# Handing out a triangular substitution's operations behind other VectorE operations, in a linear-attention kernel followed by two feed-forward layers

## The chip, the cores and the metric

One core of one Trainium2 chip runs the whole program in a single launch. The metric is the device time of one execution in microseconds (us). The engines that matter here are TensorE (PE: matmuls and, as PEld, the loading of their weights), VectorE (DVE), ScalarE (ACT), GpSimd (POOL) and SyncE (SP, which issues most DMAs). Each engine runs its own list of instructions in order and waits on semaphores for the others.

## The reference

The program computes three stages on fp32 data, cut here to what is computed:

```python
# attention: batch 4 x 8 heads, 768 positions, head size 40
for t in range(S):
    y[:, :, t] = einsum('bhd,bhde->bhe', rt, state)
    Sa = einsum('bhde,bhe->bhd', state, at)
    state = state*wt[:, :, None, :] - einsum('bhd,bhe->bhde', Sa, bt)
    state = state + einsum('bhd,bhe->bhde', vt, kt)
# mixture of experts: 3072 tokens x 320, 8 experts of width 1024, the best one of each token
h = maximum(x[mask] @ w1[e], 0);  out[mask] = gate_w * sigmoid(x @ w_output_gate)[e] * (h @ w2[e])
# shared layer of width 2048
h = x @ w_in;  g = maximum(h,0) + alpha*minimum(h,0);  out = g @ w_out
```

## The kernel before, in words

**Attention in chunks.** The recurrence is done in 12 chunks of 64 positions, and each chunk in two halves of the heads: 24 steps (`NST=24`), each for 8 groups of heads on 128 partitions. `slot(s)` writes the instructions of step s, for s from 0 to 24. Within a chunk the term `Sa` depends on earlier positions of the same chunk, so each step needs the inverse of a unit lower triangular matrix. The kernel inverts its two 32x32 diagonal blocks and joins them by matmuls.

**What is prepared ahead.** `LA=8` steps before a step runs, `stepA1` and `stepA1b` prepare its operands on VectorE: two scans over 520 columns (`F`, L604, and `e`, L610), a reciprocal and a copy of 8 columns (L607, L608), and two products (`kf`, 1024 columns, L614; `g`, 512 columns, L619). TensorE then forms `L` from them (L628). ScalarE evicts the parts of `L` to be inverted into `nt` (L633, L634), and VectorE the masked rest into `ka` (L636; `kx` in some steps, which is the same thing).

**The substitution.** Every fourth step `inv_push` (L656) takes the four steps that are complete and inverts all of their blocks at once. A stream transpose (L659) puts the blocks into `S`, so that each partition holds one 32x32 matrix. Then 30 operations `op(j)`, j from 30 down to 1, eliminate one column each: a product into `tmp` (L673, `mul` below) and an addition into `S` (L674, `add` below) over j(31-j) columns, 30 to 240. The addition needs the product, and the next operation's product needs the addition. Where j(31-j) is above 70, product and addition are each cut into two halves of rows, so that a half's successor is not the instruction that needs it. A last stream transpose writes the result `tt` (L677). Six groups of four steps are inverted: group 0 before step 0, group 1 pushed in step 0, and groups 2 to 5 at the end of steps 3, 7, 11 and 15. A group's result is first used four steps later at most, by the matmuls `W` (L744).

**How its operations are dealt out before.** `inv(n)` (L649) is called at fixed places of a step with shares from `NI=[0,1,4,1,1]`; each call issues its share of the operations that are left, all of them behind each other. In a step the places are: behind the first `W` (where s is no multiple of 4), between the two parts of the recurrence's output and the second `W` (two calls), and at the step's end.

**The rest of a step on the engines' lists.** TensorE runs, in order: `R` (L733), the transposes `XT` (L762), a part of `MY` (L772), the first `W`, the first `Pp` (L776), `R` again (L796), the second `Pp`, `MTp` (L804), the second `W`, then `MY` (L816) in two parts, of which the second needs the second `x`. Behind them come, in two of four steps, the transposes `xtp` of the finished positions (L123), and then `R` (L692), `kbp` (L642) and `L` (L628) for later steps. VectorE runs: the two `x` products from the two `Pp` (L777), some substitution operations, the state update `tm` and `mc` (L719, L720), the two output products `yt` (L821), where there is an `xtp` its small sums `lg` (L124), then `stepA1`, `stepA1b`, `ka`. ScalarE evicts `xtp` into `xu` (behind `lg`), then `kbp` into `kb`, which the next step's `R` (L733) waits for. In steps 17 to 24 no operand is prepared any more.

**What follows.** The attention's output is routed to experts while the recurrence runs, and the two feed-forward layers follow on TensorE (`hp`, L390, and `yp`, L417) from about 400 us to the end.

## Time and profile before

| | |
|---|---|
| runs, us | 1007.9, 1003.08, 1009.45 (median 1007.9) |
| profiled execution, us | 1002.83 (span of its trace 1001.1) |
| mean granted TensorE clock | 0.971 of full speed |
| TensorE busy | 938.4 us (94%) |
| VectorE busy | 778.5 us (78%), 1898 instructions |
| ScalarE busy | 397.8 us (40%) |
| chain that ended last | PE 66%, DVE 22%, DMA 5%, issue 4%, ACT 2% |

The busy shares are means over stages with different limits: attention with its prelude fills about the first 400 us of the span, the two layers the rest. The chain that ended last is followed back from the last instruction; a line's share in it says how much of the span that line's work stood on the path that set the end. In timelines one row is a run of equal instructions: start, time from the first's start to the last's end, engine, line, output<-inputs, partitions x columns, count, and in brackets how long the engine was idle before and who ended it. Since instructions overlap, the difference of two rows' starts is what the first one costs its engine.

### The profile page before, as it was taken

The page shows a single profiled execution, that of the slowest core. Times are in us where ns is not written, and L with a number is a line of the kernel's source. Part 1 is how long each engine was busy: PE and PEld are TensorE (multiplying, and loading weights), DVE is VectorE, ACT ScalarE, POOL GpSimd, SP SyncE. Part 2 cuts the span into 40 slices and gives each one's busy share as a digit, 9 for nine tenths or more (in the row PEclk, how much of TensorE's full clock was granted, in tenths as well). Part 3 has the DMA queues.
Part 4 walks back from the last instruction along what each step waited for, and adds up shares of the span by engine and source line. Part 5 has one row for each costly group of instructions (what it writes and reads, how often), then busy time and mean ns, then how long its engine had stood idle before and what let it go on. Part 6 is the DMA issues. An engine that isn't in the chain of part 4 may idle for free.

```text
span 1001.1 us, 26895 instructions
## 1 busy us (share of the span) xinstructions
PE 938.4 (94%) x11172; PEld 855.0 (85%) x11172; DVE 778.5 (78%) x1898; ACT 397.8 (40%) x816; POOL 155.0 (15%) x242
## 2 busy tenths in 40 slices
PE   5368999899999999999999999899999999999998
PEld 5367888788888898999999999778999999999997
DVE  7999999999988835788888886677666666666654
ACT  3734545445453344465555655332121212212111
POOL 1000000101110113414444443301001010100000
PEclk8568999999999999999999999999999999999999
DMA  4333867444441364467777767420001000000000
GB/s 129 117 102 103 251 215 230 117 122 126 115 118 54 97 189 130 165 231 246 226 238 230 218 230 229 146 87 27 27 1 53 1 27 27 27 27 1 28 1 26
DMA packets 59391, 118.46 MB, mean 118 GB/s; under 512 B 7492, under 2 KB 34308, under 8 KB 59268
## 3 DMA queue, kind: packets, MB, share of 16 engines
q1 hardware_dynamic: 55220, 103.04, 33.6%
q0 software_dynamic: 4048, 13.69, 4.1%
q8 instruction: 88, 1.44, 0.6%
q14 instruction: 35, 0.29, 0.1%
HBM read 90.24 MB, written 26.46 MB: 117 GB/s over the span
## 4 chain that ended last, share of the span: by engine, by line
PE 66%; DVE 22%; DMA 5%; issue 4%; ACT 2%; POOL 0%; SPq 0%; DVEq 0%; ACTq 0%; POOLq 0%
PE hp L390 24%; PE yp L417 24%; DVE S L674 4%; DVE tmp L673 4%; PE MY L816 3%; PE Pp L776 3%; DVE F L604 2%; DVE kf L614 2%; PE tp L379 2%; PE W L744 2%; DVE x L777 1%; PE MY L772 1%; DVE w L306 1%; PE R L733 1%; PE xtp L123 1%
## 5 line engine op out<-in xcount | busy, mean ns | idle before, releaser
L390 PE MATMUL hp<-xh,w 128*128 128x512 f32 (+3 forms) x1008 | 298.4, 379 | 0.1
L417 PE MATMUL yp<-w,hh 128*128 128x320 f32 (+1 forms) x1280 | 284.4, 309 | 1.0 <-ACT hh L406 0.6
L417 PEld LDWEIGHTS yp<-w,hh 128*128 128x128 f32 (+1 forms) x1280 | 217.0, 186 | 12.9 <-ACT hh L406 2.3
L390 PEld LDWEIGHTS hp<-xh,w 128*128 128x128 f32 x1008 | 187.4, 188 | 25.8 <-issue 0.4
L417 PE MATMUL yp<-w,hl 128*128 128x320 f32 x584 | 181.4, 311 | 4.1 <-DVE hl L398 3.0
L406 ACT CAST hh<-g 128x512 fp32r<-128x512 f32 x96 | 59.5, 620 | 275.4 <-PE yp L417 148.3
L390 PE MATMUL hp<-xl,w 128*128 128x512 f32 (+3 forms) x336 | 126.1, 375 | 0.2 <-DVE xl L382 0.2
L407 DVE TENSOR_TENSOR hl<-g,hh 128x512 fp32r<-128x512 f32 x96 | 66.5, 692 | 72.8 <-ACT hh L406 72.8
L417 PEld LDWEIGHTS yp<-w,hl 128*128 128x128 f32 x584 | 109.7, 188 | 6.7 <-DVE hl L398 3.8
L404 DVE TENSOR_SCALAR g<-hp,al 128x512 f32<-128x512 f32 x96 | 71.9, 749 | 39.7 <-PE hp L390 39.7
L306 DVE TENSOR_TENSOR w<-raw,w 128x1024 fp32r<-128x1024 f32 (+3 forms) x65 | 88.5, 1363 | 15.8 <-ACT w L305 14.0
L674 DVE TENSOR_TENSOR S<-S,tmp 128x110 f32<-128x110 f32 (+19 forms) x336 | 69.7, 246 | 0.8
L673 DVE TENSOR_TENSOR tmp<-S 128x110 f32<-128x110 f32 (+19 forms) x336 | 69.4, 245 | 0.5
L405 DVE SCALAR_TENSOR_TENSOR g<-hp,g 128x512 f32<-128x512 f32 x96 | 66.4, 692 | 3.3
L390 PEld LDWEIGHTS hp<-xl,w 128*128 128x128 f32 x336 | 63.4, 189 | 5.4 <-DVE xl L382 0.6
L305 ACT CAST w<-raw 128x1024 fp32r<-128x1024 f32 (+1 forms) x66 | 64.2, 974 | 5.5 <-DMA raw<-W 5.5
L504 POOL DMA_INDIRECT xg<-xs,pos x24 | 25.5, 1062 | 226.8 <-PE tp L379 167.6
L776 PE MATMUL Pp<-rz,xt 128*128 128x128 f32 x384 | 55.3, 287 | 0.0
L816 PE MATMUL MY<-x,kb 128*64 128x104 f32 (+1 forms) x768 | 43.7, 255 | 10.4 <-DVE x L777 10.4
L747 ACT COPY x<-W 32x320 f32<-32x320 f32 x96 | 40.0, 416 | 29.9 <-PE W L744 27.2
L395 ACT ACTIVATE hh<-hp 128x448 fp32r<-128x448 f32 (+2 forms) x72 | 36.6, 508 | 37.2 <-issue 25.0
L816 PEld LDWEIGHTS MY<-x,kb 128*64 128x64 f32 x768 | 36.7, 140 | 14.1 <-DVE x L777 13.0
(171 smaller groups left out, 1376.9 us busy)
## 6 DMA issues: line engine op xcount, KB each, us to landing
raw<-W SPq DMA_DIRECT2D x45, 512.0 KB
x<-VX SPq DMA_DIRECT2D x48, 232.0 KB
fm<-FM SPq DMA_DIRECT2D x46, 160.0 KB
xs<-z SPq DMA_DIRECT2D x5, 1440.0 KB
raw<-WI SPq DMA_DIRECT2D x10, 512.0 KB
raw<-WO SPq DMA_DIRECT2D x10, 512.0 KB
vv<-VM SPq DMA_DIRECT2D x24, 160.0 KB
rz<-R SPq DMA_DIRECT2D x48, 80.0 KB
```

The costliest lines, as they stand in the source:

```text
L305: s.nc.scalar.copy(hi,r[0][:,0:n])
L306: (eng or s.nc.vector).tensor_tensor(lo,r[0][:,0:n],hi.bitcast(F32),SUB)
L390: for i,(l,r) in enumerate(seq): nc.tensor.matmul(hp,l,r,start=(i==0),stop=(i==len(seq)-1))
L404: nc.vector.tensor_scalar(g,hp,0.0,s.al[:,f:f+1],ALU.min,MUL)
L405: nc.vector.scalar_tensor_tensor(g,hp,0.0,g,ALU.max,ADD)
L406: nc.scalar.copy(hh,g)
L407: nc.vector.tensor_tensor(hl,g,hh.bitcast(F32),SUB)
L417: nc.tensor.matmul(yp[j][o],l,r[:,f],start=(f==0 and i==0),stop=(f==nf-1 and i==len(p)-1))
L673: V.tensor_tensor(t3[:,r],S[:,r,j:j+1].to_broadcast([P,n,w]),S[:,j:j+1,j+1:].to_broadcast([P,n,w]),MUL)
L674: for r in rows: V.tensor_tensor(S[:,r,j+1:],S[:,r,j+1:],t3[:,r],ADD)
L776: nc.tensor.matmul(Pp[:,2*qq:2*qq+2],xt[:,qq,128*sd:128*sd+128],rz1[:,:,qq,sd],start=True,stop=True)
L816: nc.tensor.matmul(MY[q//4][64*sd:64*sd+64,q//2%2,104*(q%2)+o:104*(q%2)+o+w1],kb1[:,q,64*sd:64*sd+64],x1[:,sd,q//2,128*(q%2)+o:128*(q%2)+o ...
```

## The change

- `op(j)` no longer issues its instructions. It returns two functions, `mul` and `add`, which issue the product and the addition either in halves, as before, or whole.
- A new function `tick()` takes the next of these functions and issues it whole. It is called behind VectorE operations of other kinds: four times in `stepA1` (behind `F`, behind the copy, behind `e`, behind `kf`), once in `stepA1b` (behind `g`), behind `ka`, behind the state update `mc`, behind each `yt` and behind each `x`. These are 11 calls per step; where nothing is left to hand out, a call does nothing.
- What the calls of the remaining steps can't take, `due(r)` issues in halves, at one place per step between the second `x` and the state update, where before the two calls of `inv` stood; in the fourth step of a group it issues all that is left. The first steps of the prelude call `inv(4)` in place of `inv(8)`, since the calls of `tick` take a part there as well.
- The last group (pushed at the end of step 15) keeps halves and shares: `left[0]=25` turns `tick` off, and `share` issues 5, 2 and 1 shares at three places of a step, where before the calls of `inv` had 1+4, 1+1 and 1. In three of its four steps the single share moves behind the second `R`, `x` and `rh`.

The number of `tmp` and `S` instructions per group was 112 in all six; it is now 94, 80, 78, 78, 78 and 112, which is 152 fewer of 672. The columns that they work on are the same. The lists of TensorE, ScalarE, GpSimd and SyncE hold the same rows in the same order as before.

The core of the diff:

```diff
         nc.vector.tensor_tensor_scan(F[:,519::-1],f[:,520:0:-1],ones1.rearrange("p q t -> p (q t)")[:,::-1],0.0,MUL,ADD)
         F3=F[:,0:520].rearrange("p (q t) -> p q t",q=8)
+        tick()
...
         nc.vector.tensor_copy(e64,F3[:,:,0:1])
+        tick()
         e=ring.tile([P,8,65],F32,tag="e",name="e",bufs=LA+2)
...
+        tick()
         if s in (1,3,5): kf=xt.rearrange("p a (b h t) -> p (a b) h t",b=2,h=2)
...
         KF[s]=kf;E[s]=e;E64[s]=e64
+        tick()
...
         nc.vector.tensor_tensor(g,A3,e[:,:,0:64],MUL)
+        tick()
...
-    left=[1]; WARM=12
+    invq=deque(); fine=[]; end=[]; WARM=12
+    def tick():
+        if left[0]: return
+        if not fine and invq: fine.extend(invq.popleft())
+        if fine: fine.pop(0)(False)
     def inv(n):
-
-        l=max(left[0],n,1) if n<100 else n
-        left[0]-=n
-        for _ in range(-(-len(invq)*n//l)): invq.popleft()()
+        while fine: fine.pop(0)(False)
+        for _ in range(min(n,len(invq))):
+            for f in invq.popleft(): f(True)
         if not invq and end: end.pop()()
-    end=[]
+    def due(r): inv(100 if r==3 else max(0,-(-(len(invq)-11*(3-r)//2)//(4-r))))
+    left=[0]
+    def share(n):
+        l=max(left[0],n,1); left[0]-=n
+        inv(-(-len(invq)*n//l))
...
-            w=31-j
-            t3=ep.tile([P,240],F32,tag="tmp",name="tmp",bufs=2)[:,0:j*w].rearrange("p (a b) -> p a b",a=j)
-
-            rows=[slice(j//2,j),slice(0,j//2)] if j*w>70 else [slice(0,j)]
-            for r in rows:
-                n=r.stop-r.start
-                V.tensor_tensor(t3[:,r],S[:,r,j:j+1].to_broadcast([P,n,w]),S[:,j:j+1,j+1:].to_broadcast([P,n,w]),MUL)
-            for r in rows: V.tensor_tensor(S[:,r,j+1:],S[:,r,j+1:],t3[:,r],ADD)
+            w=31-j; t3=[]
+            def parts(split): return [slice(j//2,j),slice(0,j//2)] if split and j*w>70 else [slice(0,j)]
+            def mul(split):
+                t3.append(ep.tile([P,240],F32,tag="tmp",name="tmp",bufs=2)[:,0:j*w].rearrange("p (a b) -> p a b",a=j))
+                for r in parts(split):
+                    n=r.stop-r.start
+                    V.tensor_tensor(t3[0][:,r],S[:,r,j:j+1].to_broadcast([P,n,w]),S[:,j:j+1,j+1:].to_broadcast([P,n,w]),MUL)
+            def add(split):
+                for r in parts(split): V.tensor_tensor(S[:,r,j+1:],S[:,r,j+1:],t3[0][:,r],ADD)
+            return [mul,add]
...
-        for j in range(30,0,-1): invq.append(lambda j=j: op(j))
+        for j in range(30,0,-1): invq.append(op(j))
...
-        inv(NI[0])
         if B: wmm(0)
...
-        if s%4: inv(NI[1])
...
+        if s>=LATE and s%4: share(1)
         if Y: pp(1)
...
-        inv(NI[1])
-        inv(NI[2])
+        if s<LATE: due(s%4)
+        else: share(5)
         if B: wmm(1)
...
         if n2 is not None: a2ka(n2)
-        inv(NI[3])
+        if s>=LATE: share(2)
         if n2 is not None: loadAn()
-        inv(NI[4])
-
-        if n2 is not None and n2%4==3: inv_push(n2//4)
+        if n2 is not None and n2%4==3:
+            inv_push(n2//4)
+            if s+1==LATE: left[0]=25
```

`LATE` is 16. The other calls of `tick` stand behind `ka` (`a2ka`), behind the state update (`state`), behind each `x` (`pp`) and behind each `yt` (in `slot`); in the prelude `inv(8)` becomes `inv(4)` at two places.

How the list of VectorE moves, at the end of step 8 (the first of a group's four), from the state update to `ka`. In these rows `tmp` and `S` are the substitution's, and the numbers behind names are buffers. Before:

```order
L719 TENSOR_TENSOR tm<-MY,mc_117 128x160 x2
L720 TENSOR_TENSOR mc_117<-tm,e_1160 128x8x40
L821 TENSOR_TENSOR yt<-MY,e 128x4x64 x2
L124 TENSOR_REDUCE lg<-xtp 128x16 x2
L604 SCALAR_TENSOR_TENSOR F<-fm_91,ones_92 128x520
L607 RECIPROCAL d_93<-F 128x8
L608 COPY e_3417<-F 128x8
L610 SCALAR_TENSOR_TENSOR e<-fm_91,d_93 128x520
L614 TENSOR_TENSOR kf<-fm_91,F 128x1024
```

This stretch held no substitution operation; seven of them stood ahead of `tm`, and four more follow behind `ka`.

The same stretch of VectorE's list now:

```order
L734 TENSOR_TENSOR tm<-MY,mc_117 128x160 x2
L735 TENSOR_TENSOR mc_117<-tm,e_1129 128x8x40
L686 TENSOR_TENSOR tmp<-S 128x150
L837 TENSOR_TENSOR yt<-MY,e 128x4x64
L688 TENSOR_TENSOR S<-S,tmp 128x25x6
L837 TENSOR_TENSOR yt<-MY,e 128x4x64
L686 TENSOR_TENSOR tmp<-S 128x168
L124 TENSOR_REDUCE lg<-xtp 128x16 x2
L604 SCALAR_TENSOR_TENSOR F<-fm_91,ones_92 128x520
L688 TENSOR_TENSOR S<-S,tmp 128x24x7
L608 RECIPROCAL d_93<-F 128x8
L609 COPY e_3329<-F 128x8
```

Whole products and additions stand one by one between the others: three of them are ahead of `lg` and `F`, where none was.

VectorE's list further on, in step 9, around the two `x` products (`ez` and `sc` belong to the routing). Before:

```order
L673 TENSOR_TENSOR tmp<-S 128x110 x2
L674 TENSOR_TENSOR S<-S,tmp 128x10x11 x2
L187 SCALAR_TENSOR_TENSOR ez<-ez,sm 128x4
L188 RECIPROCAL sc<-ez 128x4
L777 TENSOR_TENSOR x_112<-Pp,mask 128x4x2x64
L673 TENSOR_TENSOR tmp<-S 128x120
L673 TENSOR_TENSOR tmp<-S 128x108
L674 TENSOR_TENSOR S<-S,tmp 128x10x12
L674 TENSOR_TENSOR S<-S,tmp 128x9x12
L673 TENSOR_TENSOR tmp<-S 128x117 x2
L674 TENSOR_TENSOR S<-S,tmp 128x9x13 x2
L777 TENSOR_TENSOR x_112<-Pp,mask 128x4x2x64
```

Two operations in halves, eight instructions, stood between the two `x`.

The same stretch now:

```order
L642 TENSOR_TENSOR kx_104<-L,mask 128x512
L686 TENSOR_TENSOR tmp<-S 128x210
L187 SCALAR_TENSOR_TENSOR ez<-ez,sm 128x4
L188 RECIPROCAL sc<-ez 128x4
L793 TENSOR_TENSOR x_112<-Pp,mask 128x4x2x64
L688 TENSOR_TENSOR S<-S,tmp 128x21x10
L793 TENSOR_TENSOR x_112<-Pp,mask 128x4x2x64
L686 TENSOR_TENSOR tmp<-S 128x220
L688 TENSOR_TENSOR S<-S,tmp 128x20x11
L686 TENSOR_TENSOR tmp<-S 128x120
L686 TENSOR_TENSOR tmp<-S 128x108
```

The first `x` now follows `ka` at once but for one product, one addition stands between the two `x`, and behind the second come one whole operation, in one piece, and three in halves.

## Rows read from the trace of the kernel before

**Rows 1.** The page: the chain that ended last, by engine, and the costliest groups:

```profile
PE 66%; DVE 22%; DMA 5%; issue 4%; ACT 2%; POOL 0%; SPq 0%; DVEq 0%; ACTq 0%; POOLq 0%
...
L674 DVE TENSOR_TENSOR S<-S,tmp 128x110 f32<-128x110 f32 (+19 forms) x336 | 69.7, 246 | 0.8
L673 DVE TENSOR_TENSOR tmp<-S 128x110 f32<-128x110 f32 (+19 forms) x336 | 69.4, 245 | 0.5
```

**Rows 2.** Busy time in a stretch: PE, PEld, DVE, ACT, POOL, PEclk, DMA:

```profile
182.00:241.00 59.00, 54.39 (x1258) 48.12 (x1251) 57.90 (x200) 28.19 (x73) 8.44 (x18) 1.00 0.44 124
```

**Rows 3.** Waits (total us, times, longest): VectorE 31 to 297; TensorE 64 to 120, 178 to 297:

```profile
DVE S L659 <- ACT nt L634: 0.8, 1, 0.8
...
PE MY L816 <- DVE x L777: 3.0, 3, 1.7
...
PE MY L816 <- DVE x L777: 6.4, 8, 1.7
```

**Rows 4.** Timeline of VectorE in step 9:

```profile
206.91 0.47 DVE L674 TENSOR_TENSOR S<-S,tmp 128x128 f32<-128x128 f32 x2
207.30 0.47 DVE L673 TENSOR_TENSOR tmp<-S 128x119 f32<-128x119 f32 x2
...
209.82 0.75 DVE L821 TENSOR_TENSOR yt<-MY,e 128x256 f32<-128x256 f32 x2
210.49 0.35 DVE L124 TENSOR_REDUCE lg<-xtp 128x16 f32<-128x64 f32 x2
210.75 1.23 DVE L604 TENSOR_TENSOR_SCAN F<-fm,ones 128x520 f32<-128x520 f32 x1
212.02 0.21 DVE L607 RECIPROCAL d<-F 128x8 f32<-128x8 f32 x1
...
212.26 1.24 DVE L610 TENSOR_TENSOR_SCAN e<-fm,d 128x520 f32<-128x520 f32 x1
213.42 1.20 DVE L614 TENSOR_TENSOR kf<-fm,F 128x1024 f32<-128x1024 f32 x1
214.53 0.69 DVE L619 TENSOR_TENSOR g<-fm,e 128x512 f32<-128x512 f32 x1
```

**Rows 5.** Timeline of VectorE, instructions that need the one before:

```profile
247.80 0.21 DVE L674 TENSOR_TENSOR S<-S,tmp 128x30 f32<-128x30 f32 x1
248.05 0.22 DVE L673 TENSOR_TENSOR tmp<-S 128x58 f32<-128x58 f32 x1
```

**Rows 6.** Timeline of TensorE, from step 12's `MY` to step 13's:

```profile
247.72 1.64 PE L816 MATMUL MY<-x,kb 128*64 128x104 f32 x30 [0.21 <-DVE x L777]
...
253.42 1.51 PE L628 MATMUL L<-g,kf 64*64 64x64 f32 x64
255.00 1.13 PE L733 MATMUL R<-mc,g 64*64 64x40 f32 x32
...
259.96 1.16 PE L776 MATMUL Pp<-rz,xt 128*128 128x128 f32 x8
...
264.15 1.64 PE L816 MATMUL MY<-x,kb 128*64 128x104 f32 x30 [1.57 <-DVE x L777]
```

**Rows 7.** Timeline of ScalarE in the same step:

```profile
253.22 0.76 ACT L126 COPY xu<-xtp 128x320 f32<-128x320 f32 x2 [5.95 <-DVE lg L124]
253.85 1.09 ACT L646 COPY kb<-kbp 128x512 f32<-128x512 f32 x2
```

**Rows 8.** Timelines of ScalarE and VectorE around the push of group 1:

```profile
72.35 0.86 ACT L747 COPY x<-W 32x320 f32<-32x320 f32 x2 [2.54 <-PE W L744]
74.39 0.37 ACT L633 ACTIVATE nt<-L 32x256 f32<-32x256 f32 x1 [1.19 <-DVE ka L636]
...
75.19 2.08 DVE L659 STREAM_TRANSPOSE S<-nt 128x1024 f32<-128x1024 f32 x1 [0.83 <-ACT nt L634]
```

**Rows 9.** Timelines of TensorE and VectorE in step 1, second `Pp` and second `x`:

```profile
86.26 1.16 PE L776 MATMUL Pp<-rz,xt 128*128 128x128 f32 x8
...
90.97 0.68 DVE L777 TENSOR_TENSOR x<-Pp,mask 128x512 f32<-128x512 f32 x1
```

More of the change, by code (lines that the diff above doesn't have):

```diff
@@ L635, in a2ev, with a2ka @@
         nc.scalar.copy(n01[b0:b0+32],L[b0:b0+32,0,:,32:64])
-    def a2ka(s): nc.vector.tensor_tensor(kas[s%LA],LP[s][:,1],mask.unsqueeze(1).to_broadcast([P,8,64]),MUL)
+    def a2ka(s):
+        nc.vector.tensor_tensor(kas[s%LA],LP[s][:,1],mask.unsqueeze(1).to_broadcast([P,8,64]),MUL)
+        tick()
     def a2kbp(s):
@@ L646, in a2kb @@
         for h in range(2): fence[0]=nc.scalar.copy(kb[:,4*h:4*h+4],r[h])
-    invq=deque()
-    left=[1]; WARM=12
+    invq=deque(); fine=[]; end=[]; WARM=12
[3 more added lines that the diff above has]
+        if fine: fine.pop(0)(False)
     def inv(n):
-        l=max(left[0],n,1) if n<100 else n
-        left[0]-=n
-        for _ in range(-(-len(invq)*n//l)): invq.popleft()()
+        while fine: fine.pop(0)(False)
+        for _ in range(min(n,len(invq))):
+            for f in invq.popleft(): f(True)
         if not invq and end: end.pop()()
-    end=[]
+    def due(r): inv(100 if r==3 else max(0,-(-(len(invq)-11*(3-r)//2)//(4-r))))
[3 more added lines that the diff above has]
+        inv(-(-len(invq)*n//l))
     def inv_push(k):
         S=ep.tile([P,32,32],F32,tag="S",name="S",bufs=1); V=nc.vector
-        inv(100); left[0]=sum(NI)*4+NI[1]*3-NI[2]-NI[3]-NI[4]
+        inv(100)
         V.transpose(out=S.rearrange("p r t -> p t r"),in_=NT[k].rearrange("p a q t -> p t (a q)"))
@@ L720, in state @@
         nc.vector.tensor_tensor(mc[:,:,0:40],tm,E64[s+2].to_broadcast([P,8,40]),MUL)
+        tick()
     lateq=[]
@@ L777, in pp @@
                 nc.vector.tensor_tensor(p4(x1[:,sd]),Pp.rearrange("p (a j) t -> p a j t",j=2),mask.unsqueeze(1).unsqueeze(1).to_broadcast([P,4,2,64]),MUL)
+                tick()
                 if s>=NST-2 and sd==0: m.spread(x1[0:1,0,0,0:1])
@@ L822, in slot @@
                 if n2 is None: fence[0]=i
+                tick()
                 if b==0: m.spread(yt[0:1,0,64*(c1%2):64*(c1%2)+1])
@@ L868, in route @@
         for _ in range(min(n,len(rq))): rq.popleft()[1]()
-    NI=[0,1,4,1,1]
     def heat(n):
@@ L886, in attention @@
     loadB(0); loadB(1)
-    inv_push(0); left[0]=8*(LA-3)
+    inv_push(0)
     a2kb(3,kbp[3])
@@ L890, in attention @@
     loadX(0); loadR(0)
-    inv(8)
+    inv(4)
     for s in range(4,LA):
@@ L897, in attention @@
         if s<LA-1: stepA1(s+1); stepA1b(s+1); loadAn(); a2ka(s)
-        inv(8)
+        inv(4)
     clear(xt); loadVT(0); loadX(1); loadR(1)
```

## The prediction

> **What bounds the kernel now.** I read the chain of waits first: TensorE holds 66% of it and VectorE 22%, and the two lines of the substitution, 672 instructions, are the costliest of VectorE [rows 1]. The feed-forward layers are TensorE's; the change touches VectorE's list in the attention alone, so the attention has to be read by itself. Steps 8 to 11 take 59.0 us, VectorE is busy for 57.9 of them, TensorE for 54.4, at a granted clock of 1.00, which is the 2.4 GHz level [rows 2]. Who waits decides it: from 31 to 297 us VectorE waits for another engine once, 0.8 us, while TensorE waits for VectorE's `x` 3.0 us in steps 1 to 3 and 6.4 us in steps 8 to 15 [rows 3]. So from the first push to step 15 VectorE's list is the time, and an instruction less on it is worth its spacing, as far as TensorE's list is not met underneath: there is room for some 3 us per group of four steps, not for more.
>
> **What a merged pair saves.** Spacing, not duration, is the price, since instructions overlap. `kf`, 1024 columns, costs 1.11 us, from 213.42 to 214.53; the two `yt` of 256 cost 0.67, 0.335 each [rows 4]. That is 1.01 ns per column and 0.077 us per instruction. Two halves with 240 columns together cost 206.91 to 207.30, 0.39 us [rows 4]; which is what this price gives (2x0.077+0.242), although the substitution's rows are short and spaced; whole they should cost 0.077+0.242=0.32. A merged pair saves 0.07. No substitution instruction in this trace has over 128 columns, so the bounds are nothing (if longer strided rows run slower) and 0.077 (the whole fixed cost); I take 0.07, since `yt` and `kf` lie on either side of 240 columns. 152 instructions fewer: 10.6 us, of which 18 in group 0, 32 in group 1 and 34 in each of groups 2 to 4 (2.4 us a group).
>
> **Waits inside VectorE.** An instruction that needs the one before it starts 0.25 us behind it even at 30 columns [rows 5], against 0.077+0.03: a wait of 0.14. Such waits stand behind `F` (1.27 to the reciprocal, where `e`, equally long, costs 1.16: 0.11) and before `e` (0.24 for the two short ones, 2x0.085 without a wait: 0.07) [rows 4]. Operations handed out there fill 0.18, in 3 rounds of the prelude and 12 steps: 2.7 us. But wholes also come to stand behind each other: in two steps of each of groups 2 to 4 a product, its addition and the next product are in a row, two waits of 0.14, 1.7 us, and a few more in group 1 and in the prelude. I count both as even. VectorE's list so gets 10.6 us shorter.
>
> **A rule against it.** Halves start 0.19 us apart, and two of them last 0.47 from the first's start to the second's end, so one lasts 0.28 [rows 4]: an instruction starts before its predecessor ends, if it doesn't need it. The Trainium skill, "VectorE: DVE Perf Modes", section "The DRAIN you can't avoid", says that the next operation does not start until the pipe is empty, and that only the number of operations counts. By it nothing would be filled, and a removed instruction would be worth the whole distance between dependent ones, 0.22 us beyond its columns: 152 of them 33 us. The rows here speak against that rule; it gets no chance of its own.
>
> **What of the 10.6 us reaches the end.** Three places take some back.
>
> *Push of group 1.* The transposition at 75.19 waits for `nt`, whose eviction at 74.39 waits for `ka`; but ScalarE's copies of `x` before it end at 72.35+0.86=73.21 [rows 8], behind matmuls that hang on the prelude's last `ka`, which now comes no earlier (nine operations stand ahead of it whole, but also two more in all). So `nt` can come 0.8 us earlier rather than the 1.4 that VectorE gains in group 0: 0.6 lost.
>
> *Step 1.* The second `x` at 90.97 is 15.8 us behind that transposition; its `Pp` ends at 86.26+1.16=87.42 [rows 8, 9]. In the new order the addition of operation 23 and operations 22 to 18 come behind this `x`: 2364 columns and 22 instructions, 4.1 us; seven merges and a filled wait make 0.7 more. VectorE would be there after 11.0 us, at 85.4, and `Pp`, 0.8 earlier than before, ends at 86.6: 1.2 lost.
>
> *First to second step of groups 2 to 4.* From `MY` to `MY` the step took 16.43 us, all of it VectorE's, with TensorE waiting 1.57 for `x` [rows 6]. Three operations (20, 19, 18: 12 instructions and 1364 columns, 2.3 us) and a product (0.25) move to later steps, ten merges save 0.7 and a filled wait 0.2: 13.0 us. TensorE takes from `MY` at 247.72 to the end of the second `Pp` at 261.12, 13.4 us, and `x` to `MY` 0.65 more [rows 6]. Some 0.4 of this goes: `L` is stretched to 1.51 because `R` at 255.00 waits for ScalarE's `kb` copies, which end at 254.94 behind `xu`, which waited for VectorE's `lg` [rows 6, 7]; now the three operations between `tm` and `lg` delay it by 0.75, but `tm` itself comes over 1.5 us earlier, four operations in halves instead of seven being ahead of it. So 13.65 against 13.0, 0.65 lost, somewhat more in step 4 to 5, where VectorE's list is shorter: 2.2 for the three groups. In the other steps what is saved counts: over the group VectorE's list, 59.0-2.4=56.6 us, stays above TensorE's 54.4 [rows 2].
>
> Together 10.6-0.6-1.2-2.2=6.6 us; I take 7. Behind step 15 nothing else changes but the place of a single share in three steps of the last group, which then has VectorE waiting and TensorE busy; I cost it at nothing, and 0.3 either way. The feed-forward layers start earlier by what the attention gains: their weights are loaded at places of the same list, and the other engines' lists are unchanged. The profiled execution took 1002.8, so 995.8; it stands at the fast end of the runs shown, whose median of 1007.9 would give 1000.9. I forecast 998, between the two.
>
> **The rivals.**
>
> *A: VectorE alone counts.* If TensorE's list closes up (the stretched `L`, the short waits between matmuls), the 10.6 arrive, and something of the filled waits: 992 from the profiled execution, 997 from the median. For it speaks that TensorE's waits for `x` add up to 9.4 us in two of the three stretches [rows 3]; against it that they lie in the first two steps of a group and the savings in all. 0.20.
>
> *B: the chain over ScalarE takes the place.* `lg`, `xu`, `kb`, `R` [rows 7] hang behind three more operations between `tm` and `lg`. If `tm` is then held by `MY` and not by VectorE's list, each of the six steps with `xtp` (the first two of groups 2 to 4) loses the 0.75 that stand ahead of `lg`: 4.5 us less, a gain of 2.5, 1000 from the profiled execution and 1005 from the median. Against it: behind the second `x` (0.6) the operations due in halves take over 2 us, while `MY` is through 0.65+1.64=2.3 us behind the start of `x` [rows 6]. 0.15.
>
> *C: slower, by holding.* If an operation that stands between others of another shape waits for them, or they for it, as dependent ones do, each of some 160 handed out costs 0.14: 22 us against 10.6, 1014 from the profiled execution. It decides at 10.6/160=0.066 us per handed-out operation. The spacing of 0.335 between the two `yt` and 0.67 to the sums behind them [rows 4] shows no such hold between operations of different kinds. 0.05.
>
> *D: it does nothing.* The whole operations cost what their halves do, because a row of several columns and a hop to the next costs more than a row of contiguous ones. Against it: the halves, cut the same way, cost what the price of `kf` and `yt` gives [rows 4]. 1003 from the profiled execution, 1008 from the median. 0.04.
>
> *Forecast:* a gain of 4.5 to 9 us, 0.56.
>
> **Numbers.** Bounds of the forecast: 1002.8-9=994 and 1007.9-4.5=1003. The range of 991 to 1004 takes in A and most of B; it leaves out C, the slow end of B and D. About 1%, 10 us, can be told from no change here. The forecast's 7 is below that, but the runs shown are 6 us apart and the median is at their slow side, so a part of the forecast and most of A come out as faster by over 1%: 0.36. Within 1%: the rest of the forecast, B and D: 0.59. Slower by over 1%: C, 0.05.
>
> **What would show it.** In the changed trace: a whole operation of 240 columns costs 0.32 to the next instruction (D: 0.39; C: 0.45 or more). 520 instead of 672 substitution instructions. Group stretches like steps 8 to 11 take 57 us instead of 59.0 (A: 56.5; B: 58.5). VectorE waits for `Pp` before the second `x` of steps 1, 5, 9 and 13, by 0.5 to 1.2 us, where it waited for nothing; TensorE's waits for `x` shrink in those steps. In B the waits are `tm` on `MY`, and TensorE's `R` on `kb`. I am wrong if a wait longer than 1.5 us stands in any step, or if the savings in the group stretches don't show in the start of the feed-forward layers.

## The result, and the profile after

The changed kernel takes 996.0 us (median of 7 runs, 993.2 to 998.7), the kernel before beside it 1005.3 (7 runs, 1002.7 to 1009.6): ratio 0.9902, interval 0.9877 to 0.9927, so 9.9 us faster, between 7.3 and 12.4 (the two medians lie 9.3 apart). The forecast was 998 in a range of 991 to 1004, with a gain of 7. In the profiled executions the span went from 1001.1 to 991.4 us; that of the changed kernel is the fastest of its seven runs.

The page of the changed kernel, its chain by engine and the two groups of the substitution, which answer to [rows 1] (line, operation, count, busy us, mean ns, idle before):

```profile
PE 70%; DVE 17%; DMA 5%; issue 4%; ACT 4%; SPq 0%; POOL 0%; ACTq 0%; DVEq 0%; POOLq 0%
...
L686 DVE TENSOR_TENSOR tmp<-S 128x120 f32<-128x120 f32 (+28 forms) x260 | 64.0, 272 | 1.1
L688 DVE TENSOR_TENSOR S<-S,tmp 128x120 f32<-128x120 f32 (+28 forms) x260 | 63.8, 271 | 1.0
```

520 instructions instead of 672, and VectorE's share of the chain fell from 22% to 17%. The 127.8 us that the two groups are still busy are only 11.3 less, since the columns are the same ones.

The stretch that answers to [rows 2], steps 8 to 11, in the same columns:

```profile
177.00:234.30 57.30, 53.11 (x1266) 47.55 (x1264) 55.40 (x166) 28.12 (x74) 9.34 (x18) 1.00 0.46 128
```

57.3 us instead of 59.0, VectorE busy for 55.4 in 166 instructions, where it was 57.9 in 200; granted clock 1.00 in both.

The waits that answer to [rows 3] (total us, times, longest): first VectorE from 31 to 290 us:

```profile
DVE x L793 <- PE Pp L792: 3.3, 3, 2.0
DVE S L672 <- ACT nt L639: 1.6, 1, 1.6
```

Then TensorE from 172 to 288 us:

```profile
PE W L760 <- ACT rh L752: 3.2, 4, 1.1
PE MY L832 <- DVE x L793: 3.1, 4, 1.7
PE R L749 <- ACT kb L653: 0.8, 2, 0.6
```

VectorE, which waited once, now waits four times, and TensorE's waits for `x` fell from 6.4 to 3.1. In the groups of steps 8 to 15 each of the two lists now meets the other once. Not all that TensorE no longer waits for `x` is won: in this stretch `W` waits 3.2 us for `rh`, ScalarE's negated copy of `R`, where it was 1.6 before, and from 64 to 116 us 4.7, where it was 1.4 from 64 to 120 before.

VectorE's timeline in step 9 (start, duration, instruction, idle before), which answers to [rows 4]:

```profile
198.19 0.69 DVE L793 TENSOR_TENSOR x<-Pp,mask 128x512 f32<-128x512 f32 x1 [0.77 <-PE Pp L792]
198.80 0.38 DVE L686 TENSOR_TENSOR tmp<-S 128x220 f32<-128x220 f32 x1
199.21 0.39 DVE L688 TENSOR_TENSOR S<-S,tmp 128x220 f32<-128x220 f32 x1
199.63 0.46 DVE L686 TENSOR_TENSOR tmp<-S 128x120 f32<-128x120 f32 x2
...
202.91 0.40 DVE L686 TENSOR_TENSOR tmp<-S 128x240 f32<-128x240 f32 x1
203.24 0.42 DVE L837 TENSOR_TENSOR yt<-MY,e 128x256 f32<-128x256 f32 x1
203.57 0.40 DVE L688 TENSOR_TENSOR S<-S,tmp 128x240 f32<-128x240 f32 x1
203.88 0.42 DVE L837 TENSOR_TENSOR yt<-MY,e 128x256 f32<-128x256 f32 x1
204.22 0.40 DVE L686 TENSOR_TENSOR tmp<-S 128x240 f32<-128x240 f32 x1
204.53 0.35 DVE L124 TENSOR_REDUCE lg<-xtp 128x16 f32<-128x64 f32 x2
```

Whole operations of 240 columns stand between others at 202.91, 203.57 and 204.22, and the next one starts 0.33, 0.31 and 0.31 us later: the 0.32 of the prediction. Where a whole addition follows its own product, at 199.21, it starts 0.41 behind it and the next product 0.42 behind that, 220 columns each: 0.077+0.222 without a wait, so a wait of 0.11 to 0.12, where the prediction had 0.14. The first row shows VectorE waiting for the second `Pp`, as forecast for this step.

Where the 9.7 us of the two traces arise (start of the instruction, us):

| place | before | after | saved |
|---|---|---|---|
| transposition at the push of group 1 | 75.19 | 74.26 | 0.9 |
| second `x` of step 1 | 90.97 | 85.35 | 5.6 |
| second `x` of step 4 | 129.24 | 126.24 | 3.0 |
| second `x` of step 8 | 187.95 | 184.37 | 3.6 |
| second `x` of step 12 | 246.98 | 241.63 | 5.3 |
| transposition at the push of the last group | 300.76 | 293.30 | 7.5 |
| first matmul of the feed-forward layers | 407.27 | 398.07 | 9.2 |
| end of the span | 1001.1 | 991.4 | 9.7 |

The last group begins 7.5 us earlier; another 1.7 come behind it up to the feed-forward layers, where the prediction expected nothing, and 0.5 in those layers. Of the 5.6 us at step 1 a part is only moved: between the push and this `x` stand 1640 columns of the substitution instead of 4004, and the other 2364 come behind it. So the saving falls to 3.0 by step 4. The same happens within a group: the first step, from second `x` to second `x`, fell from 16.43 to 13.82 us, while the other three together took 43.4 instead of 42.6.

### The profile page after: what moved, and what is told of

It reads as the page before. It is cut to its first block, busy times and chain, and to the rows that moved or that the text cites. A ratio compares the mean times of both kernels' runs of the same rounds, so it can differ in the third digit from the quotient of the medians.

```text
span 991.4 us, 26738 instructions
## 1 busy us (share of the span) xinstructions
PE 932.2 (94%) x11172; PEld 850.9 (86%) x11172; DVE 766.6 (77%) x1746; ACT 397.4 (40%) x816; POOL 155.4 (16%) x242
## 4 chain that ended last, share of the span: by engine, by line
PE 70%; DVE 17%; DMA 5%; issue 4%; ACT 4%; SPq 0%; POOL 0%; ACTq 0%; DVEq 0%; POOLq 0%
PE hp L390 25%; PE yp L417 25%; PE Pp L792 3%; DVE tmp L686 3%; PE MY L832 3%; DVE S L688 2%; PE W L760 2%; PE tp L379 2%; DVE F L604 2%; PE R L749 1%; PE R L707 1%; PE xtp L123 1%; PE MY L788 1%; DMA x<-VX 1%; PE L L633 1%
## 5 line engine op out<-in xcount | busy, mean ns | idle before, releaser
L686 DVE TENSOR_TENSOR tmp<-S 128x120 f32<-128x120 f32 (+28 forms) x260 | 64.0, 272 | 1.1
L688 DVE TENSOR_TENSOR S<-S,tmp 128x120 f32<-128x120 f32 (+28 forms) x260 | 63.8, 271 | 1.0
L793 DVE TENSOR_TENSOR x<-Pp,mask 128x512 f32<-128x512 f32 x48 | 32.8, 685 | 21.6 <-PE Pp L792 21.5
L792 PEld LDWEIGHTS Pp<-rz,xt 128*128 128x128 f32 x384 | 46.4, 191 | 2.5 <-ACT xu L126 0.2
```

Of the source, the lines that this page charges most:

```text
L686: V.tensor_tensor(t3[0][:,r],S[:,r,j:j+1].to_broadcast([P,n,w]),S[:,j:j+1,j+1:].to_broadcast([P,n,w]),MUL)
L688: for r in parts(split): V.tensor_tensor(S[:,r,j+1:],S[:,r,j+1:],t3[0][:,r],ADD)
L792: nc.tensor.matmul(Pp[:,2*qq:2*qq+2],xt[:,qq,128*sd:128*sd+128],rz1[:,:,qq,sd],start=True,stop=True)
```

## Experiments

Ratios are against the kernel before, run beside it on the same chip. "Group" is the distance of the second `x` of step 8 to that of step 12 in the profiled execution, 59.0 before and 57.3 after. A step's time is the distance from its second `x` to the next step's; in brackets behind it stands that of the changed kernel.

### Merging or handing out: e1 and e2

e1 is the changed kernel with halves handed out:

```diff
-        if fine: fine.pop(0)(False)
+        if fine: fine.pop(0)(True)
...
-        while fine: fine.pop(0)(False)
+        while fine: fine.pop(0)(True)
```

> The changed kernel, but every operation that is handed out is issued in halves, as before; places, order and columns are those of the change. Theory (fewer instructions are the gain, 0.07 us each): 152 instructions come back, 10.6 us on VectorE's list; some 2.5 of it fall into the waits that VectorE now has in step 1 and in steps 5, 9, 13, and the waits between two whole operations in a row go. So 6 to 8 us slower than the changed kernel, 1002 to 1004 if that one stands at 996, 1 to 3 us faster than before; steps 8 to 11 take 58.5 to 59 us. Rival (the gain is the filled waits behind F and e and the even spread over the steps): 996 to 998, steps 8 to 11 stay at 57.3.

Measured: 1000.4 us, ratio 0.9967 (0.9945 to 0.9989); group 59.4; second `x` of step 15 at 289.9, where it stands at 291.2 before and at 283.2 in the changed kernel. VectorE's timeline of e1 between the two `yt` of step 9:

```profile
207.16 0.47 DVE L686 TENSOR_TENSOR tmp<-S 128x120 f32<-128x120 f32 x2
207.55 0.42 DVE L837 TENSOR_TENSOR yt<-MY,e 128x256 f32<-128x256 f32 x1
207.88 0.47 DVE L688 TENSOR_TENSOR S<-S,tmp 128x120 f32<-128x120 f32 x2
208.27 0.42 DVE L837 TENSOR_TENSOR yt<-MY,e 128x256 f32<-128x256 f32 x1
```

Two halves with 240 columns cost 0.39 wherever they stand. By this trace handing out alone is worth 1.3 us of the 8.0 at step 15, and merging the other 6.7. But the trace has something that the first one of the changed kernel has not: TensorE's granted clock fell in step 8 (columns of [rows 2]):

```profile
187.90:191.30 3.40, 3.20 (x32) 2.77 (x31) 2.93 (x17) 0.00 (x0) 0.00 (x0) 0.50 0.02 5
```

From step 8 to 9 it took 14.80 us, from 12 to 13, where the clock stayed, 13.68. Without these 1.1 us the group takes 58.2, handing out alone is worth 2.4 at step 15, and merging 5.6. By the times merging is worth 6.5 us (0.9967 against 0.9902), and what handing out brings by itself can't be told from nothing, since the last group's part (e4 below) is in e1 too.

e2 is the kernel before with whole operations in their old places:

```diff
-            rows=[slice(j//2,j),slice(0,j//2)] if j*w>70 else [slice(0,j)]
+            rows=[slice(0,j)]
```

> The kernel before with every operation whole, at its old places, one behind the other; 52 instructions fewer per group. Theory: each whole operation waits 0.14 us for the one before, and saves 0.077 us for a merged pair; 52x(0.14-0.077)=3.3 us more per group in groups 0 to 4, nothing in the last group, which doesn't bound: 12 to 17 us slower than before, 1017 to 1022. Rival (only the number of instructions counts, as the Trainium skill's section on the drain has it; an instruction never overlaps the next): 52x0.22=11 us less per group, until TensorE bounds at some 54 us per group: 20 us or more faster, 985 or less.

Measured: 1013.1 us, ratio 1.0087 (1.0057 to 1.0118); group 60.9. Second `x` of step 15 at 302.3, 11.1 us later than before. VectorE's timeline where products and additions of 240 columns follow each other:

```profile
214.12 0.41 DVE L673 TENSOR_TENSOR tmp<-S 128x240 f32<-128x240 f32 x1
214.56 0.41 DVE L674 TENSOR_TENSOR S<-S,tmp 128x240 f32<-128x240 f32 x1
215.00 0.41 DVE L673 TENSOR_TENSOR tmp<-S 128x240 f32<-128x240 f32 x1
215.44 0.41 DVE L674 TENSOR_TENSOR S<-S,tmp 128x240 f32<-128x240 f32 x1
```

0.44 us apart, where the two halves of [rows 4] cost 0.39: what the merge saves, the wait takes, and more. So merging alone loses: it needs something else between an operation and the one that needs it. The step is 0.077+0.242 and a wait of 0.12. It is slower by 8.7 us (5.7 to 11.8), less than the 12 to 17 expected; the group lost 1.8 us in the trace and not 3.3. The rule of the Trainium skill that the prediction weighed ("VectorE: DVE Perf Modes", "The DRAIN you can't avoid"), that the next operation does not start until the pipe is empty, would have made e2 faster, by fewer instructions; it is 8.7 us slower, so here the measurement decides against it. The same section of the Trainium skill adds that a next operation that is not held starts earlier, which the prediction left out; the halves of [rows 4], 0.19 apart and 0.28 long, do that.

### The last group: e3, e4 and e8

e3 is the changed kernel with the last group dealt out as before: the single share of steps 17 to 19 ahead of `R`, and the other calls split again:

```diff
+        if s>=LATE and s%4: share(1)
...
-        if s>=LATE and s%4: share(1)
...
-        else: share(5)
+        else: share(1); share(4)
...
-        if s>=LATE: share(2)
+        if s>=LATE: share(1)
...
+        if s>=LATE: share(1)
```

> The changed kernel with the last group dealt out exactly as before, the single share of steps 17 to 19 ahead of the second R and of x again. In the trace of the changed kernel 1.2 us more are saved between step 15's second x and the first matmul of the feed-forward layers (114.9 us against 116.1). Theory T (the clock): before, TensorE waited 1.8 us for yt at the start of step 17, and its clock then stood at 1.2 GHz for 3.4 us; after it waited 1.2 us and the clock stayed. If the moved share shortened that wait, this kernel has the wait of 1.8 us back and the stretch takes 115.5 to 116.1 us; 996.5 to 997.5 in all. Rival (the moved share does nothing; the clock fell by chance of the moment): 114.9 us with the full clock, 996.

Measured: 998.6 us, ratio 0.9944 (0.9917 to 0.9971); second `x` of step 15 at 282.9.

e4 is the kernel before with the last group dealt out as in the change, which also joins calls:

```diff
-        if s%4: inv(NI[1])
+        if s<LATE and s%4: inv(NI[1])
...
+        if s>=LATE and s%4: inv(NI[1])
...
-        inv(NI[1])
-        inv(NI[2])
+        if s<LATE: inv(NI[1]); inv(NI[2])
+        else: inv(NI[1]+NI[2])
...
-        inv(NI[3])
+        inv(NI[3] if s<LATE else NI[3]+NI[4])
...
-        inv(NI[4])
+        if s<LATE: inv(NI[4])
```

> The kernel before with nothing but the last group's single share moved behind the second R, x and rh, as in the change. If the moved share is worth the time behind step 15, the stretch from step 15's second x to the first matmul of the feed-forward layers takes 114.9 to 115.4 us instead of 116.1, and the whole 1004 if the kernel before stands at 1005.3; if it does nothing, 116.1 and 1005.3 (or 114.7 if the clock happens not to fall). Steps 1 to 15 as before: 59.0 us for steps 8 to 11.

Measured: 1001.2 us, ratio 0.9960 (0.9936 to 0.9985); second `x` of step 15 at 291.4, as before.

The parts add up: 5.6 us (2.9 to 8.3) without the last group's change and 4.0 (1.5 to 6.4) with it alone, 9.6 of 9.9. What was changed in the last group is less the place of the single share than the joining of calls. In VectorE's list the single share of step 17 stands between the two `x` in both kernels, eight instructions long. But a call rounds its share of the operations up: 1 and 4 of 25 shares, taken one after the other, issue 2 and 5 of the 30 operations, and 5 in one call issue 6. The instructions on `S` between the second `x` and `tm` in steps 16 and 17 (us, VectorE busy and count, POOL, clock, DMA), first before, then in the changed kernel:

```profile
305.90:310.37 4.47, 3.59 (x24) 0.00 (x0) 1.00 0.30 73
320.90:325.02 4.12, 3.85 (x20) 0.00 (x0) 1.00 0.16 46
```

```profile
298.40:302.24 3.84, 2.95 (x20) 0.00 (x0) 1.00 0.23 55
311.40:316.09 4.69, 4.59 (x24) 0.00 (x0) 1.00 0.21 46
```

One operation, four instructions, has gone from step 16, ahead of the `yt` that step 17's `R` waits for, to step 17; e4 has the lists of the changed kernel here, e3 those of the kernel before. What this does, TensorE's timeline shows at the start of step 17; first e3, then the stretch behind it (columns of [rows 2]):

```profile
303.60 1.13 PE L749 MATMUL R<-mc,gx 64*64 64x40 f32 x32 [1.79 <-DVE yt L837]
...
305.06 1.97 PE L788 MATMUL MY<-rz,mt 128*64 128x128 f32 x16
```

```profile
305.00:315.00 10.00, 10.00 (x108) 8.98 (x104) 4.86 (x23) 2.08 (x6) 0.09 (x1) 0.50 0.06 18
```

The same in the changed kernel:

```profile
304.05 1.13 PE L749 MATMUL R<-mc,gx 64*64 64x40 f32 x32 [1.17 <-DVE yt L837]
...
305.51 1.09 PE L788 MATMUL MY<-rz,mt 128*64 128x128 f32 x16
```

```profile
305.50:315.50 10.00, 10.00 (x213) 9.12 (x209) 7.67 (x38) 3.66 (x9) 0.02 (x1) 1.00 0.13 41
```

With the calls split as before `R` waits 1.79 us for `yt`, as it did before, and now 1.17: 0.6 us. By itself this is worth less. From the last push to step 18's `R` the changed kernel takes 24.60 us, and e8 below, which has the old split and no fall of the clock here, 24.86: the operation is only put off to step 17, and step 18's `R` then waits 0.3 for `yt`. Behind the wait of e3 the granted clock is 0.50, the 1.2 GHz level, and `MY` takes 1.97 instead of 1.09; from the push to step 18's `R` it takes 29.5, so this fall costs 4.7. The fall behind the same wait of the kernel before was a short one: 26.4 us, 1.5 more than without. Over all profiled executions: behind a wait of 1.79 us or more the clock fell in three of three, behind one of 1.16 or 1.17 in three of seven, behind 0.65 or less in none of four. So, as far as these few traces show it, the last group's gain is a fall that comes less often, and not the 0.6 us of waiting.

e8 tests the clock's part on the kernel before, with five matmuls whose result is not used:

```diff
+            if s==LATE+1: heat(5)
             R1=R1s.pop(s)
```

> The kernel before with five matmuls of the identity by itself (some 1 us, results not used) ahead of step 17's first matmul R, where TensorE waited 1.79 us for yt before its granted clock fell to 1.2 GHz. Theory 1 (the moved share of the last group gained by keeping the clock): the wait is filled by half, no clock fall behind it, second x of step 15 to the feed-forward layers 114.5 to 115 instead of 116.1, time 2 to 4 us below the kernel before, ratio 0.996 to 0.998. Theory 2 (it gained by the shorter wait itself, and the clock's part is small): the wait for yt ends as late as before, ratio 0.9995 to 1.0005, tail 115.8 or more. The five matmuls do not delay R if they end inside the wait.

TensorE's timeline of e8, the start of step 17:

```profile
309.10 1.31 PE L875 MATMUL warm<-ident 128*128 128x128 f32 x10
311.06 1.13 PE L734 MATMUL R<-mc,gx 64*64 64x40 f32 x32 [0.65 <-DVE yt L822]
...
312.52 1.09 PE L773 MATMUL MY<-rz,mt 128*64 128x128 f32 x16
```

The five matmuls are ten rows. The wait is filled but for 0.65 us and `MY` takes 1.09. Behind step 15 this trace is 2.5 us shorter (113.6 for 116.1), 0.8 of it ahead of the last push, where the two kernels do not differ, and 1.8 behind it. But the time is 1002.1 us, ratio 0.9995 (0.9976 to 1.0014): over many executions keeping the clock at this one place is worth 2.4 us at most. Theory 1 has its mechanism in the trace, and its size is at the upper edge of what the times allow; theory 2's ratio fits and its trace doesn't. So of the last group's 4.0 us (1.5 to 6.4) the operation put off explains 0.3 and the clock up to 2.4. The intervals meet between 1.5 and 2.7 us; that the clock is all of it is not shown.

### What binds now: e5, e6 and e7

e5 issues one operation more in the first step of a group:

```diff
-    def due(r): inv(100 if r==3 else max(0,-(-(len(invq)-11*(3-r)//2)//(4-r))))
+    def due(r): inv(100 if r==3 else max(0,-(-(len(invq)-11*(3-r)//2)//(4-r)))+(r==0))
```

> The changed kernel with one more whole operation issued in the first step of every group (and so one less in a later step). The step from r0 to r1 has VectorE waiting for Pp at its end (0.77 us in step 9), so one operation more (0.6 us) should be hidden there. Theory 1 (TensorE's list sets that step): from second x to second x it stays 13.8 us, steps 8 to 12 take 56.7 instead of 57.3, x of step 15 comes 1.5 us earlier, the time is 994 to 995, ratio to the kernel before 0.988. Theory 2 (the chain lg, xu, kb, R behind VectorE's lg sets it; the operation does not stand ahead of lg in that step, but what follows it in the list does): the step grows to 14.2 to 14.4, steps 8 to 12 stay at 57.3, time 996, ratio 0.990.

Measured: 993.7 us, ratio 0.9914 (0.9883 to 0.9946); step 8 to 9 14.06 (13.82), step 10 to 11 12.20 (12.84), group 56.8. The operation is hidden for the most part: 0.24 of its 0.6 us shows, and 0.64 goes from the third step. Nearer to theory 1 in the group, but `x` of step 15 comes at 283.2, as in the changed kernel and not 1.5 us earlier, with a fall of the clock in step 12 to 13 (14.83); the gain can't be told from the changed kernel's by the time.

e6 keeps handed-out operations away from the places ahead of `lg` in steps with `xtp` (`due` issues what is then left):

```diff
-        tick()
+        if not ready: tick()
...
-                tick()
+                if not ready: tick()
...
+            if u: s.tick()
```

> The changed kernel with the sums lg ahead of the operations handed out in the two steps of a group that have xtp: nothing is handed out behind mc and the two yt there, one operation behind the second lg. If the chain lg, xu, kb, R holds the step from r0 to r1 (rival B of the prediction): R starts 0.3 to 0.45 us earlier, L is stretched less than 1.57, r0 to r1 takes 13.4 to 13.55 instead of 13.8, steps 8 to 12 56.6 to 56.9 instead of 57.3, time 994 to 995 (ratio 0.988 to 0.989). If VectorE's and TensorE's lists hold it: no step is shorter, up to three operations less a step are handed out and their waits of 0.11 come back, steps 8 to 12 57.3 to 57.8, time 996 to 998 (0.990 to 0.992).

Measured: 997.4 us, ratio 0.9934 (0.9901 to 0.9967); the steps without a fall of the clock got longer, 9 to 10 15.24 (15.13) and 10 to 11 13.14 (12.84). The step from 8 to 9, which the expectation speaks of, had a fall in it (15.04), so by itself it shows nothing; the same step of the group before, from 4 to 5, had none and took 14.84 (14.76). No step is shorter, which speaks against the chain over ScalarE.

e7 hands out behind the routing's short instructions too, and between `tm` and `mc`, and issues as many fewer in `due` (two of the places):

```diff
-            V.tensor_tensor(rk,rk,oh,MUL)
-            pf=s.pf[:,n0:n1]; V.tensor_reduce(pf,rk,AX.X,ADD)
+            V.tensor_tensor(rk,rk,oh,MUL); s.tick()
+            pf=s.pf[:,n0:n1]; V.tensor_reduce(pf,rk,AX.X,ADD); s.tick()
...
+        tick()
         nc.vector.tensor_tensor(mc[:,:,0:40],tm,E64[s+2].to_broadcast([P,8,40]),MUL)
-        tick()
```

> The changed kernel with operations also handed out behind the short dependent instructions of the routing (mx, d, v, m2; le; the running ranks rk, pf, m2; the sums zz and sm; ez) and between tm and mc instead of behind mc, and as many fewer in the due parts. If dependent waits of about 0.11 us are what is left in VectorE's list, some 18 are filled and some 14 between a product and its addition go: up to 3.5 us a group less on VectorE. Theory 1 (VectorE's list still sets the later steps of a group; TensorE's 54.4 us and its stretches are met after 1.5 to 2.3 us): steps 8 to 12 55.0 to 55.8 instead of 57.3, time 990 to 992, ratio 0.985 to 0.987. Theory 2 (TensorE's list is met already): steps 8 to 12 57.0 or more, time 995 to 997, ratio 0.990 to 0.991.

Measured: 997.4 us, ratio 0.9929 (0.9904 to 0.9954), no better than the changed kernel; group 56.6, with a fall of the clock in it, and three more at 114.6, 244.3 and 305.7 us. The steps without one are shorter: 9 to 10 14.55 (15.13), 10 to 11 12.20 (12.84).

### Keeping the clock: e9 to e12

e9 is e5, and e10 is e7, each with unused matmuls in TensorE's waits:

```diff
+            if s==LATE+1: heat(3)
...
         if B: wmm(1)
+        if 0<s<LATE and s%4==0: heat(5)
```

> e5 (one operation more in the first step of a group) with matmuls of the identity, results not used, in TensorE's waits: five (1.3 us) behind the second W of steps 4, 8 and 12, where TensorE waits 1.7 to 1.9 us for x, and three (0.8 us) ahead of step 17's R, where it waits 1.2 us for yt. Theory 1 (what is left between executions is the granted clock, which falls in or behind those waits): no fall between 95 and 320 us in the profile, the times closer together (993 +- 1.5), median 992 to 993, ratio 0.988 to 0.990. Theory 2 (the falls come from elsewhere, or cost little): falls still there, median 994 to 996, ratio 0.990 to 0.993. If the five end behind x, steps 4, 8 and 12 grow by what they are late.

> e7 (operations handed out in the routing too) with the same matmuls of the identity in TensorE's waits (five behind the second W of steps 4, 8 and 12, three ahead of step 17's R). In e7 the clock fell to 1.2 GHz at 114.6, 186.3, 244.3 and 305.7 us, each behind a wait of TensorE of 1.2 to 1.95 us, while the steps without a fall were shorter (r1 to r2 14.55 for 15.13, r2 to r3 12.20 for 12.84). Theory 1 (the falls took what the shorter list of VectorE had saved): no falls there, steps 8 to 12 54.8 to 55.6, x of step 15 at 279 to 281, time 988 to 991, ratio 0.984 to 0.988. Theory 2 (TensorE's list and its waits for ScalarE are met): steps 8 to 12 56.3 or more without a fall, time 994 to 996, ratio 0.990 to 0.993.

Measured: e9 997.4 us, ratio 0.9928 (0.9902 to 0.9954); in step 8 the five matmuls waited themselves for the buffer that `x` frees, 1.84 us, and stood in front of `MY`; between 95 and 320 us one fall was left, at 102.5, and the ratio is theory 2's. e10 993.7 us, ratio 0.9902 (0.9870 to 0.9933); no fall between 71 and 627 us, group 56.15, second `x` of step 15 at 281.0. So the filled waits of VectorE are worth 1.1 us per group on top of the changed kernel, not the 1.7 to 2.5 of theory 1; the five matmuls wait in step 8 here too, 1.99 us. The ratio is the changed kernel's. VectorE's timeline of e10 in the routing shows that handing out there works, starts 0.11 to 0.13 us apart, with two chains side by side:

```profile
237.89 0.20 DVE L687 TENSOR_TENSOR tmp<-S 128x30 f32<-128x30 f32 x1
238.00 0.19 DVE L168 TENSOR_TENSOR v<-v,ohs 128x32 f32<-128x32 f32 x1
238.12 0.21 DVE L689 TENSOR_TENSOR S<-S,tmp 128x30 f32<-128x30 f32 x1
238.24 0.18 DVE L169 TENSOR_REDUCE pf<-v 128x4 f32<-128x32 f32 x1
238.37 0.22 DVE L687 TENSOR_TENSOR tmp<-S 128x58 f32<-128x58 f32 x1
```

e11 is e7 with three matmuls in W's spare columns and three ahead of step 17's `R`, and one operation moved from the second step of a group to the first (against e7); e12 is the changed kernel, beside it:

```diff
-    def due(r): inv(100 if r==3 else max(0,-(-(len(invq)-(39,27,12)[r]//2)//(4-r))))
+    def due(r): inv(100 if r==3 else max(0,-(-(len(invq)-(39,27,12)[r]//2)//(4-r))+(1,-1,0)[r]))
...
+            if s==LATE+1: heat(3)
...
+                for _ in range(3 if i and 0<s<LATE and s%4==0 else 0): nc.tensor.matmul(Wt[:,320:448],ident,ident,start=True,stop=True)
```

> e7 (operations handed out in the routing too) with three matmuls of the identity behind the second W of steps 4, 8 and 12, written into W's spare columns so that they need no buffer that x frees, three ahead of step 17's R, and one whole operation moved from the second step of a group to the first, where VectorE still waits 0.74 us for Pp in e10 (and 0.99 in the third step). Theory 1 (VectorE's list sets the steps without such a wait): r0 to r1 stays 13.4 to 14.1, r1 to r2 falls from 14.55 to 14.0 to 14.3, steps 8 to 12 55.2 to 55.8 (e10 56.15), time 989 to 993, ratio 0.984 to 0.988, and below the changed kernel run beside it by 4 to 7 us. Theory 2 (TensorE's list and its waits for ScalarE set them): steps 8 to 12 56 to 56.5, time 993 to 995, 1 to 3 us below the changed kernel.

> The changed kernel as it is, once more, beside e11 on the same chip: ratio to the kernel before 0.988 to 0.993 by its first measurement, 994 to 998; x of step 15 at 283, steps 8 to 12 57.3. If the clock falls in its waits too (step 17's R, 1.2 us; x of step 8, 1.7 us), the profile shows a fall that the first one did not, and what it costs.

Measured: e11 994.3 us, ratio 0.9895 (0.9861 to 0.9930); e12 994.8, ratio 0.9914 (0.9884 to 0.9943). They can't be told apart: no version here is shown to beat the changed kernel. The group of e11, 56.0 us without a fall, lies between the two theories. Its step 9 to 10 stayed at 14.53, where theory 1 wanted 14.0 to 14.3, so VectorE's list no longer sets that step. e12 had two falls that the first trace did not have, in steps 8 and 12. TensorE's timeline at step 8, first e12 and its stretch, then the first trace of the same kernel:

```profile
184.60 3.59 PE L832 MATMUL MY<-x,kb 128*64 128x104 f32 x32 [1.75 <-DVE x L793]
```

```profile
184.60:188.00 3.40, 3.30 (x32) 2.97 (x32) 3.05 (x18) 0.00 (x0) 0.00 (x0) 0.51 0.07 21
```

```profile
184.40 0.39 PE L832 MATMUL MY<-x,kb 128*64 128x104 f32 x2 [1.74 <-DVE x L793]
185.10 1.64 PE L832 MATMUL MY<-x,kb 128*64 128x104 f32 x30 [0.31 <-DVE x L793]
```

The same `MY` behind the same wait (1.75 and 1.74 us) takes 3.59 us at a clock of 0.51, or is through 2.34 us after its start at the full clock. The two falls, 0.86 us in step 8 to 9 and 1.07 in step 12 to 13, are nearly all of the 2.1 us by which e12's second `x` of step 15 comes later than in the first trace. So what reaches the last push in the changed kernel, 7.5 us in the first trace, is 6.2 in this one.

## Why the prediction was right, and what was off

*The bound.* VectorE's list set the time up to step 15: with the same columns in fewer instructions the last group begins 7.5 us earlier (6.2 in e12), and TensorE's waits for `x` halved. The sum of the prediction up to there was 6.6.

*The price of a merged pair.* 0.32 us for 240 whole columns was forecast, 0.31 to 0.33 measured. Rival D (0.39) falls with it, and rival C: an operation of another shape between two others, even one that is needed two places on, costs no more than its columns and 0.077.

*The waits, counted as even.* Nearly: in e1, where no whole operation stands behind another, handing out is worth 1.3 us at step 15, 2.4 without the fall of the clock (2.7 in the prediction), and the waits left between wholes of 220 and 240 columns cost 0.11 to 0.12 each, not the 0.14 of 30 columns. What the prediction did not say is how much hangs on them: without the handing out the merge loses (e2, 8.7 us slower).

*What is taken back.* At the push of group 1 VectorE waits 1.6 us for `nt` instead of 0.8; 0.6 lost was forecast, it is 0.8. From the first to the second step of groups 3 and 4 13.82 and 13.59 us were measured, 13.65 forecast. (From the second `x` to `MY` it is 0.74, from 246.98 to 247.72, not the 0.65 of the prediction; with it 13.74.) The other steps of group 3 took 15.13, 12.84 and 15.47, where they took 15.15, 12.62 and 14.83: the operations moved there cost 2.5 us by the prediction's prices, and 0.8 of it shows, so the merges count in these steps too. The group's 57.3 stands beside the 57 forecast. Step 1 was wrong: 1.2 us should have been lost waiting for `Pp`, and nothing was, since `Pp` ended at 84.96. Instead VectorE waited for `Pp` in step 5, TensorE's timeline:

```profile
136.87 1.16 PE L792 MATMUL Pp<-rz,xt 128*128 128x128 f32 x8
137.96 0.41 PE L811 MATMUL R<-x,n 32*32 32x40 f32 x12
139.32 0.55 PE L811 MATMUL R<-x,n 32*32 32x40 f32 x20 [0.96 <-issue]
139.80 1.16 PE L792 MATMUL Pp<-rz,xt 128*128 128x128 f32 x8
```

And VectorE's:

```profile
138.67 0.37 DVE L688 TENSOR_TENSOR S<-S,tmp 128x210 f32<-128x210 f32 x1
141.00 0.69 DVE L793 TENSOR_TENSOR x<-Pp,mask 128x512 f32<-128x512 f32 x1 [1.96 <-PE Pp L792]
141.60 0.38 DVE L686 TENSOR_TENSOR tmp<-S 128x220 f32<-128x220 f32 x1
```

TensorE stood for 0.96 us inside `R` with no releaser that the profile shows (0.42 in the kernel before, at the same matmul), and VectorE waited 1.96 us for `Pp`. The same stop stands in 12 of the 14 traces here, 0.36 to 0.96 us long; its cause stays open. VectorE's wait is longer than the 1.5 that the prediction named as its own refutation; it is one place, and the sum to the last push, 7.5 against 6.6, holds.

*The step that failed* is "I cost it at nothing, and 0.3 either way", of the single share in the last group. With the last group's change alone the kernel before gets 4.0 us faster (1.5 to 6.4, e4). The step looked at a place in VectorE's list that does not move, and not at the joined calls, which take one operation from ahead of the `yt` on which step 17's `R` waits; TensorE sets that stretch. For the list alone "nothing, and 0.3 either way" is right: 0.3 us at step 18's `R` while the clock stays. What the prediction put at nothing is the clock behind that wait. In the profiled executions the change is worth 1.7 us behind the last push, about the 1.5 that the kernel before lost there by a fall and the changed kernel did not.

*Luck.* The gain of 9.9 us (7.3 to 12.4) lies above the 4.5 to 9 to which the prediction gave most weight, and what takes it there is largely this part, which was not forecast. That 996.0 lies well inside the range owes something to the range's width, which spans two bases 5 us apart.

*The rivals.* Rival A's figure of 992 to 997 fits the time as well as the forecast does, but not for its reason: 7.5 of its 10.6 us arrive at the last push, and e5, e7 and e11 show that TensorE's list is met in several steps. Rival B is not seen: group 57.3 rather than its 58.5, and e6, which takes the operations away from ahead of `lg`, gains nothing. The median of three runs that the prediction had, 1007.9, became 1005.3 with seven, which is the base of 1005 that the forecast of 998 stands on; from it the gain was 2 to 3 us larger than the 7 forecast.

## What to carry to other kernels

Where an engine's list is the bound, count an instruction by the distance to the next start, and see which waits a merge lays open: halving an operation had hidden the wait for its own result, and merging pays only with other work put in between. When something is moved on an engine that has time, ask who waits for what stands behind it, and count what the code really issues: one operation that VectorE could do at any time, there by the rounding of two calls, held TensorE for 0.6 us, and behind the longer wait its clock fell in three traces of three. And when two lists are within 2 or 3% of each other, filling the one further buys little; the experiments that did so took VectorE from 55.4 to 53.7 us a group and no measurable time.

## What the runs showed of the hardware that was not expected

- Two dependent instructions of VectorE in a row cost 0.11 to 0.12 us beyond their columns and 0.077; one other instruction between them, even a short one, takes that away. The rows of e10 start 0.11 to 0.13 us apart.
- After a wait of 1.2 to 1.8 us TensorE's granted clock fell to 1.2 GHz in some executions and not in others (step 8: 1.74 us without, 1.75 with a fall, the same kernel; step 17: three of seven at 1.16 to 1.17 us, of different kernels). One fall costs from 0.86 (step 8, e12) to 4.7 us (step 17, e3 against e8).
- Where the wait was filled with unused matmuls, no fall stood behind it in the trace (e8, e10), but the time moved by nothing that could be measured in e8; they also need a buffer, and in e9 and e10 they waited for it in step 8 (1.84 and 1.99 us).
